# Summing a half's exponentials within that half's own turn of the loop

## The chip, the cores and the metric

The kernel runs on one core of one Trainium2 chip. The metric is the device time of one execution in microseconds. Three executions of the kernel before took 923.88, 924.41 and 924.57 us, a median of 924.41.

## The reference

The program is hashed attention followed by one MLP-mixer block. With 4 batches, 8 heads, 768 positions and 64 values a head, a query sees the keys whose 6-bit hash equals its own:

```python
q_bits = (np.einsum('bhsd,dk->bhsk', q, proj) > 0)
k_bits = (np.einsum('bhsd,dk->bhsk', k, proj) > 0)
mask = q_bucket[:, :, :, None] == k_bucket[:, :, None, :]
scores = np.where(mask, scale * np.matmul(q, k.transpose(0, 1, 3, 2)), -1000000000.0)
attn = np.exp(scores - np.max(scores, axis=-1, keepdims=True))
attn = attn / (np.sum(attn, axis=-1, keepdims=True) + 1e-09)
x = np.matmul(attn, v)
...
h = np.maximum(xt @ w_tok1, 0.0) @ w_tok2      # token mixing
u = x + h.transpose(0, 2, 1)
out = u + np.maximum(u @ w_ch1, 0.0) @ w_ch2   # channel mixing
```

## The kernel before

There are three stages, one behind the other: attention (to about 386 us of the profiled span), token mixing, and channel mixing. The change lies in `attention`. Each engine works through its own instructions in the order in which the code emits them, so that this order is what the change edits; waits between engines are semaphores that the framework adds from the tiles that are read and written.

Attention runs over 16 pairs of heads, `n`, and over two halves of 384 queries for each pair: 32 halves, numbered 0 to 31 here. A half's `scores` (L299) multiplies the six key blocks of 128 keys with its queries on TensorE and adds the hash bits; ScalarE turns each block into an exponential tile `e` (L306). The score banks of PSUM rotate over three buffers, which the hash products share, so that the fourth block waits until ScalarE has read the first.

`add` sums the six `e` tiles of a half. Part 0 adds `e` 0 and 1 on GpSimd into `esa` (L329) and `e` 2, 3, 4 on VectorE into `esd` (L331, L332); part 1 adds `e` 5 (L334) and then `esa` (L335) on VectorE. `sums` sends `esd` through TensorE against a tile of ones (L343); ScalarE takes Ln and Exp of the result (L347, L348), and VectorE refines the reciprocal in two instructions (L350, L351), called the refinement below. `weigh` multiplies the `e` tiles by the values on TensorE (L359), ScalarE copies the result to `num` (L364), and GpSimd multiplies it by the reciprocal into `XT` (L367).

The loop is shifted by one half: during half k (`now`) the sums and the weighing of half k-1 (`before`) run, so on TensorE the order of half k is scores of k, sums of k-1, the hash product of the next pair (L266, in the first half of a pair only), weighing of k-1. VectorE turns the hash products into bits `g` (L271, L274), and the SP queue sends them on in eight small transfers (L280), followed in that queue by the next `qk` (L240), a raw weight tile (L154) and the next values (L248, L250).

Beside all this the 64-bit mixer weights are converted, one tile of 768 columns at a time, in three thirds that are spread over three halves. Third 0, `begin`, scales the low words on ScalarE (L165) and builds the high part on VectorE (L167, L170). Third 1, `join`, masks on VectorE (L182), then multiplies and adds on GpSimd (L185, L186). Third 2, `end`, squares on ScalarE (L195), writes the weight on VectorE (L196), and fetches the next raw tile; there is one raw buffer. Eight tiles pass in the loop. A half in which third 1 is emitted is called a joining half below.

Of the kernel before, what the change touches and what calls it, by code (L numbers as in the profile page):

```python
# [48 lines left out]
def kernel(  # L49
# [169 lines left out]
    def turn(b, x, bank):  # L219

        for r in range(0, NR, 2):
            ps = bank()
            for k in range(2):
                at = S * b + P * (r + k)
                for cb in range(NCB):
                    nc.tensor.transpose(ps[:, k, P * cb : P * cb + P], XT[:, cb, at : at + P], ident)
            nc.scalar.copy(x[:, r : r + 2], ps)


    def attention(pool, psum, W1, W2, x0):  # L230
# [3 lines left out]
        def load_qk(n):  # L234
            if n >= len(pairs):
                return
            b, hp = pairs[n]
            t = pool.tile([P, 2, S], F32, name="qk", tag="qk", bufs=3)
            for sl in [slice(0, HALF), slice(HALF, S)] if n == 0 else [slice(0, S)]:
                nc.sync.dma_start(out=t[:, :, sl], in_=qk[b, hp, :, :, sl])  # L240
            loaded[n] = [t, None, None, None]

        def load_v(n):
            if n >= len(pairs):
                return
            b, hp = pairs[n]
            vn = pool.tile([P, 2, NR, D], F32, name="vn", tag="vn", bufs=3)
            nc.sync.dma_start(out=vn, in_=v[b, hp])  # L248
            vt = pool.tile([P, S], F32, name="vt", tag="vt", bufs=2)
            nc.sync.dma_start(out=vt, in_=vT[b, hp])  # L250
            loaded[n][1:3] = vn, vt

        def add_values(n):

            vt = loaded[n][2]
            vsum = pool.tile([P, 1], F32, name="vsum", tag="vsum", bufs=4)
            nc.scalar.activation(vt, vt, ACT.Copy, scale=-EPS, accum_out=vsum)
            loaded[n][3] = vsum

        def hashes(n):  # L260

            g = pool.tile([P, HALF], BF16, name="g", tag="g", bufs=2)
            ps = psum.tile([P, 2, 512], F32, name="hp", tag="sc", bufs=3)[:, 0]
            for j in range(4):
                sl = slice(HALF * (j // 2), HALF * (j // 2) + HALF)
                nc.tensor.matmul(  # L266
                    ps[32 * j : 32 * j + 32, :HALF], projblk, loaded[n][0][:, j % 2, sl],
                    start=True, stop=True,
                )
            for rows in [slice(0, 64), slice(64, P)] if n == 0 else [slice(0, P)]:  # L270
                nc.vector.tensor_scalar(  # L271
                    g[rows], ps[rows, :HALF], 0.0, 0.5, op0=ALU.is_gt, op1=ALU.subtract,
                )
                nc.vector.tensor_scalar(g[rows], g[rows], bitscale[rows], None, op0=ALU.mult)  # L274
            for j in range(4):
                sl = slice(HALF * (j // 2), HALF * (j // 2) + HALF)
                for i in range(2):
                    at = 32 * j + 16 * i
                    issuer = nc.scalar if n == 0 and i else nc.sync
                    issuer.dma_start(  # L280
                        out=zeroed[n % 3][D * i : D * i + NB + 1, j % 2, sl], in_=g[at : at + NB + 1],
                    )

        class Half:
# [54 lines left out]
            def sums(self):  # L339

                ps = psum.tile([P, 512], F32, name="sums", tag="sm", bufs=1)[:, :HALF]
                for i in range(2):
                    nc.tensor.matmul(  # L343
                        ps[D * i : D * i + D], ones, self.d[:, i], start=True, stop=True,
                    )
                near = pool.tile([P, HALF], F32, name="near", tag="near", bufs=2)
                nc.scalar.activation(near, ps, ACT.Ln)  # L347
                nc.scalar.activation(near, near, ACT.Exp, scale=-1.0)  # L348
                rec = self.rec = pool.tile([P, HALF], F32, name="rec", tag="rec", bufs=2)
                nc.vector.tensor_tensor(rec, ps, near, op=ALU.mult)  # L350
                nc.vector.scalar_tensor_tensor(rec, rec, 2.0, near, op0=ALU.subtract, op1=ALU.mult)  # L351
# [31 lines left out]
        before = None  # L383
        third = 0
        for n in range(len(pairs)):
            for half in range(2):
                now = Half(n, half)
                now.scores()
                if n == half == 0:
                    add_values(0)  # L390
                if before:
                    before.add(1)
                    before.sums()
                if half == 0 and n + 1 < len(pairs):
                    hashes(n + 1)
                    load_qk(n + 2)
                if half == 1 and n + 1 < len(pairs):
                    add_values(n + 1)
                if n:
                    weights.some(third)  # L400
                    third = (third + 1) % 3
                now.add(0)
                if before:
                    before.weigh()
                if half == 0:
                    load_v(n + 2)
                before = now
        while third or weights.fetched:
            weights.some(third)
            third = (third + 1) % 3  # L410
        before.add(1)
        turn(0, x0, lambda: psum.tile([P, 2, 512], F32, name="trp", tag="sc", bufs=3))
        before.sums()
        before.weigh()


# [318 lines left out]
    def attention_and_tokens(W1, W2, x0):  # L735
        inside(attention, W1, W2, x0)
        pool = late.enter_context(tc.tile_pool(name="late", bufs=1, side="right", reuse_waits="tile"))
        WC2 = big["WC2"] = pool.tile([P, NHT, DM], F32, name="WC2")
        SW1 = big["SW1"] = pool.tile([P, 3, NCB // 2, DCH // 2], F32, name="SW1")
        SW2 = big["SW2"] = pool.tile([P, 3, NHT // 2, DM // 2], F32, name="SW2")  # L740

        def weights(pool):
            return Conversion(
                pool, [(w_ch1, WC1, 1, (NCB // 2, NCB)), (w_ch2, WC2, 3, (0, NHT))], bufs=3,
            )

        def jobs(conversion):
            n1, n2 = (NCB // 2) * DCH // NW, NHT * DM // NW
            return [
                *[conversion.one] * (n1 + 1),  # L750
                *weight_sums(
                    WC1, SW1, slice(0, NCB // 2), slice(NCB // 2, NCB),
                    slice(0, DCH // 2), slice(DCH // 2, DCH),
                ),
                *[conversion.one] * n2,
                *weight_sums(
                    WC2, SW2, slice(0, NHT // 2), slice(NHT // 2, NHT),
                    slice(0, DM // 2), slice(DM // 2, DM),
                ),
            ]  # L760

        inside(tokens, W1, W2, x0, weights, jobs)
# [63 lines left out]
```

## Time and profile before

| what | value |
|---|---|
| median of 3 runs | 924.41 us |
| the profiled execution's own time | 924.47 us |
| its span, first to last instruction | 922.6 us |
| TensorE busy in the span | 871.5 us (94%) |
| VectorE, ScalarE, GpSimd busy | 512.3, 323.0, 261.8 us |
| mean granted TensorE clock over the span | 0.98 |

Times in the timeline are counted from the start of the span. "Idle before" is the time that an engine stood still ahead of an instruction, with the instruction that released it. A granted clock of 1.00 is 2.4 GHz; where TensorE is at the lower of its two levels, 1.2 GHz, its matmuls take about twice as long in the timeline.

### The profile page before, as it was taken

The page shows a single profiled execution, that of the slowest core. Times are in us where ns is not written, and L with a number is a line of the kernel's source. Part 1 is how long each engine was busy: PE and PEld are TensorE (multiplying, and loading weights), DVE is VectorE, ACT ScalarE, POOL GpSimd, SP SyncE. Part 2 cuts the span into 40 slices and gives each one's busy share as a digit, 9 for nine tenths or more (in the row PEclk, how much of TensorE's full clock was granted, in tenths as well). Part 3 has the DMA queues.
Part 4 walks back from the last instruction along what each step waited for, and adds up shares of the span by engine and source line. Part 5 has one row for each costly group of instructions (what it writes and reads, how often), then busy time and mean ns, then how long its engine had stood idle before and what let it go on. Part 6 is the DMA issues. An engine that isn't in the chain of part 4 may idle for free.

```text
span 922.6 us, 9203 instructions
## 1 busy us (share of the span) xinstructions
PE 871.5 (94%) x3505; PEld 397.0 (43%) x3505; DVE 512.3 (56%) x576; ACT 323.0 (35%) x477; POOL 261.8 (28%) x156
## 2 busy tenths in 40 slices
PE   5989889889889899999999999999999999999997
PEld 1434334334334444545553444444444444444443
DVE  1675776666675756558996447353446452335511
ACT  2656666666656565543421220101121101221000
POOL 3343553551651532254652111110111110111020
PEclk8999999989999999999999999999999999999999
DMA  4222222322312220221320120131110110000001
GB/s 173 72 71 106 105 71 106 104 71 105 105 71 105 71 71 3 103 69 68 118 88 1 69 69 0 58 114 65 61 68 35 57 69 34 0 1 0 23 23 49
DMA packets 20499, 61.14 MB, mean 66 GB/s; under 512 B 2784, under 2 KB 4192, under 8 KB 20448
## 3 DMA queue, kind: packets, MB, share of 16 engines
q1 hardware_dynamic: 20392, 60.46, 18.5%
q8 instruction: 29, 0.48, 0.2%
q14 instruction: 22, 0.18, 0.1%
q10 hardware_dynamic: 56, 0.02, 0.0%
HBM read 53.49 MB, written 6.29 MB: 65 GB/s over the span
## 4 chain that ended last, share of the span: by engine, by line
PE 75%; DVE 9%; POOL 7%; ACT 3%; DMA 2%; SPq 2%; issue 1%; DVEq 0%; ACTq 0%
PE b L581 46%; PE sc L299 10%; PE acc L359 8%; PE t L516 4%; PE sums L343 3%; POOL tmp L185 2%; POOL tmp L186 2%; PE t L529 2%; POOL esa L329 2%; DVE esd L335 2%; SPq L280 1%; DMA raw<-in_moe_w_tok 1%; PE hp L266 1%; DMA qk<-in_qk 1%; DVE tmp L170 1%
## 5 line engine op out<-in xcount | busy, mean ns | idle before, releaser
L306 ACT ACTIVATE e<-sc 128x768 f32<-128x768 f32 x192 | 151.8, 812 | 29.7 <-PE sc L299 29.6
L299 PE MATMUL sc<-qk 64*128 64x384 f32 x768 | 160.5, 497 | 1.0 <-ACT e L306 1.0
L588 ACT COPY p<-b 128x512 f32<-128x512 f32 x72 | 42.2, 586 | 295.5 <-PE b L581 295.5
L359 PE MATMUL acc<-e,vn 128*64 128x384 f32 x768 | 136.5, 507 | 0.0
L581 PE MATMUL b<-r,WC 128*128 128x512 f32 x288 | 125.6, 592 | 0.0
L581 PE MATMUL b<-T,SW 128*128 128x512 f32 x216 | 97.0, 593 | 1.7 <-DVE T L671 0.9
L607 POOL TENSOR_TENSOR p<-p,p 128x512 f32<-128x512 f32 x18 | 25.4, 1414 | 238.9 <-ACT p L588 228.2
L299 PEld LDWEIGHTS sc<-qk 64*128 64x128 f32 x768 | 67.5, 189 | 58.4 <-issue 47.8
L359 PEld LDWEIGHTS acc<-e,vn 128*64 128x64 f32 x768 | 56.5, 143 | 79.7 <-issue 77.9
L581 PEld LDWEIGHTS b<-r,WC 128*128 128x128 f32 x288 | 54.7, 190 | 68.9 <-issue 66.5
L367 POOL TENSOR_TENSOR XT<-num,rec 128x384 f32<-128x384 f32 x32 | 41.0, 1280 | 145.4 <-ACT num L364 141.5
L329 POOL TENSOR_TENSOR esa<-e 128x768 f32<-128x768 f32 x32 | 73.0, 2281 | 29.3 <-ACT e L306 29.3
L350 DVE TENSOR_TENSOR rec<-sums,near 128x384 f32<-128x384 f32 x32 | 17.9, 558 | 101.3 <-ACT near L348 101.3
L185 POOL TENSOR_TENSOR tmp<-tmp,raw 128x768 f32<-128x768 f32 x20 | 46.2, 2309 | 91.7 <-DVE tmp L182 54.6
L581 PE MATMUL b<-T,WC 128*128 128x512 f32 x144 | 67.7, 593 | 0.1
L299 PE MATMUL sc<-bits 64*128 64x384 bf16 x384 | 63.6, 325 | 1.3 <-DMA bits<-g 1.3
L581 PE MATMUL b<-XT,WC 128*128 128x512 f32 x144 | 64.7, 592 | 0.0
L581 PEld LDWEIGHTS b<-T,SW 128*128 128x128 f32 x216 | 40.9, 190 | 54.0 <-issue 50.5
L581 PE MATMUL b<-r,SW 128*128 128x512 f32 x144 | 62.8, 592 | 0.0
L611 DVE TENSOR_TENSOR r<-p,u 128x512 f32<-128x512 f32 x18 | 12.5, 692 | 87.6 <-ACT u L588 87.0
L343 PE MATMUL sums<-esd,ones 128*64 128x384 f32 x128 | 31.1, 568 | 28.4 <-DVE esd L335 28.4
L335 DVE SCALAR_TENSOR_TENSOR esd<-esd,esa 128x768 f32<-128x768 f32 x32 | 42.6, 1330 | 16.1 <-POOL esa L329 13.6
(81 smaller groups left out, 992.8 us busy)
## 6 DMA issues: line engine op xcount, KB each, us to landing
raw<-in_moe_w_ch SPq DMA_DIRECT2D x16, 768.0 KB
seen<-in_qk SPq DMA_DIRECT2D x16, 768.0 KB
qk<-in_qk SPq DMA_DIRECT2D x15, 768.0 KB
vn<-in_v SPq DMA_DIRECT2D x16, 384.0 KB
vt<-in_vT SPq DMA_DIRECT2D x16, 384.0 KB
out<-p SPq DMA_DIRECT2D x18, 256.0 KB
raw<-in_moe_w_tok SPq DMA_DIRECT2D x4, 768.0 KB
bits<-g SPq DMA_DIRECT2D x124, 5.2 KB
```

What stands on the lines that cost most here:

```text
L185: nc.gpsimd.tensor_tensor(unit, unit, lo, op=ALU.mult)
L299: nc.tensor.matmul(sc[:, i, :HALF], t[rows, 1, P * c : P * c + P], t[rows, 0, qs], start=start, stop=not start,)
L306: nc.scalar.activation(e, sc[:, :, :HALF], ACT.Exp, scale=SCALE)
L329: nc.gpsimd.tensor_tensor(self.a, es[0], es[1], op=ALU.add)
L335: nc.vector.scalar_tensor_tensor(self.d, self.d, NR * EPS, self.a, op0=ALU.add, op1=ALU.add,)
L343: nc.tensor.matmul(ps[D * i : D * i + D], ones, self.d[:, i], start=True, stop=True,)
L359: nc.tensor.matmul(acc[D * i : D * i + D], vn[:, i, c], e[:, i], start=(c == 0), stop=(c == NR - 1),)
L367: nc.gpsimd.tensor_tensor(XT[:, hp, at : at + HALF], num, self.rec, op=ALU.mult)
L516: nc.tensor.matmul(ps, W1[:, r, P * j : P * j + P], x[:, r], start=(r == 0), stop=(r == NR - 1),)
L581: nc.tensor.matmul(self.ps[i], left(k), right(k), start=first and k == ks[0], stop=k == ks[-1], skip_group_check=True,)
L588: nc.scalar.copy(c, self.ps[i])
L607: nc.gpsimd.tensor_tensor(p7, p5, p7, op=ALU.add)
```

## The change

`now.add(0)` moves from the end of a half's turn, behind the weight third, to a place straight behind its scores. `now.add(1)` moves from the next half's turn into the half's own: it stands behind the refinement of half k-1, ahead of the weight third. So that the refinement can be placed by itself, it is cut off `sums` into a method of its own, `newton`, which stands behind the hash bits. No instruction is added or removed.

```diff
--- before.py
+++ after.py
@@ -346,6 +346,10 @@
                 near = pool.tile([P, HALF], F32, name="near", tag="near", bufs=2)
                 nc.scalar.activation(near, ps, ACT.Ln)
                 nc.scalar.activation(near, near, ACT.Exp, scale=-1.0)
+                self.ps, self.near = ps, near
+
+            def newton(self):
+                ps, near = self.ps, self.near
                 rec = self.rec = pool.tile([P, HALF], F32, name="rec", tag="rec", bufs=2)
                 nc.vector.tensor_tensor(rec, ps, near, op=ALU.mult)
                 nc.vector.scalar_tensor_tensor(rec, rec, 2.0, near, op0=ALU.subtract, op1=ALU.mult)
@@ -388,18 +392,20 @@
                 now.scores()
                 if n == half == 0:
                     add_values(0)
+                now.add(0)
                 if before:
-                    before.add(1)
                     before.sums()
                 if half == 0 and n + 1 < len(pairs):
                     hashes(n + 1)
                     load_qk(n + 2)
                 if half == 1 and n + 1 < len(pairs):
                     add_values(n + 1)
+                if before:
+                    before.newton()
+                now.add(1)
                 if n:
                     weights.some(third)
                     third = (third + 1) % 3
-                now.add(0)
                 if before:
                     before.weigh()
                 if half == 0:
@@ -408,9 +414,9 @@
         while third or weights.fetched:
             weights.some(third)
             third = (third + 1) % 3
-        before.add(1)
         turn(0, x0, lambda: psum.tile([P, 2, 512], F32, name="trp", tag="sc", bufs=3))
         before.sums()
+        before.newton()
         before.weigh()
```

On VectorE, a joining half without a hash product and the half behind it, with one. `tmp` and `W_93` belong to the weight thirds, `rec` to the refinement, `g` to the hash bits. Before:

```order
L182 TENSOR_SCALAR tmp<-tmp 128x768
L331 TENSOR_TENSOR esd<-e 128x768
L332 TENSOR_TENSOR esd<-esd,e 128x768
L334 TENSOR_TENSOR esd<-esd,e 128x768
L335 SCALAR_TENSOR_TENSOR esd<-esd,esa 128x768
L350 TENSOR_TENSOR rec<-sums,near 128x384
L351 SCALAR_TENSOR_TENSOR rec<-rec,near 128x384
L271 TENSOR_SCALAR g<-hp 128x384
L274 TENSOR_SCALAR g<-g,bitscale 128x384
L196 SCALAR_TENSOR_TENSOR W_93<-raw,tmp 128x768
```

After (the refinement's two lines are now L354 and L355):

```order
L334 TENSOR_TENSOR esd<-esd,e 128x768
L335 SCALAR_TENSOR_TENSOR esd<-esd,esa 128x768
L182 TENSOR_SCALAR tmp<-tmp 128x768
L331 TENSOR_TENSOR esd<-e 128x768
L332 TENSOR_TENSOR esd<-esd,e 128x768
L271 TENSOR_SCALAR g<-hp 128x384
L274 TENSOR_SCALAR g<-g,bitscale 128x384
L354 TENSOR_TENSOR rec<-sums,near 128x384
L355 SCALAR_TENSOR_TENSOR rec<-rec,near 128x384
L334 TENSOR_TENSOR esd<-esd,e 128x768
L335 SCALAR_TENSOR_TENSOR esd<-esd,esa 128x768
L196 SCALAR_TENSOR_TENSOR W_93<-raw,tmp 128x768
```

Before, the joining half's four additions stand behind L182; now all four stand ahead of it, and the next half's first two stand ahead of the bits and the refinement.

On GpSimd, the same joining half with what stands ahead of it and behind it. Before:

```order
L367 TENSOR_TENSOR XT<-num,rec 128x384
L185 TENSOR_TENSOR tmp<-tmp,raw 128x768
L186 TENSOR_TENSOR tmp<-tmp 128x768
L329 TENSOR_TENSOR esa<-e 128x768
L367 TENSOR_TENSOR XT<-num,rec 128x384
L329 TENSOR_TENSOR esa<-e 128x768
```

After (L371 is the former L367):

```order
L329 TENSOR_TENSOR esa<-e 128x768
L185 TENSOR_TENSOR tmp<-tmp,raw 128x768
L186 TENSOR_TENSOR tmp<-tmp 128x768
L371 TENSOR_TENSOR XT<-num,rec 128x384
L329 TENSOR_TENSOR esa<-e 128x768
L371 TENSOR_TENSOR XT<-num,rec 128x384
```

The joining half's own addition has moved from behind the two instructions of the join to ahead of them; the addition of the half behind it still follows them. The orders of TensorE and of ScalarE are as before.

## Rows read from the trace of the kernel before

**Rows 1.** Waits, 20 to 440 us: engine, line <- releaser: total us, times, longest us
```profile
PE sums L343 <- DVE esd L335: 28.4, 12, 3.2
...
DVE esd L335 <- POOL esa L329: 13.6, 8, 1.7
```

**Rows 2.** Busy us (x instructions) of each engine by stretch, granted clock, DMA share, GB/s
```profile
28.00:323.00 295.00, 266.58 (x1698) 118.75 (x1696) 195.02 (x206) 182.34 (x268) 129.47 (x67) 0.95 0.25 91
...
323.00:374.00 51.00, 51.00 (x344) 23.30 (x340) 28.93 (x34) 33.98 (x51) 16.45 (x11) 1.00 0.10 34
...
199.00:209.00 10.00, 6.82 (x32) 2.06 (x30) 5.50 (x7) 4.13 (x6) 6.26 (x4) 0.68 0.01 2
```

**Rows 3.** Timeline of TensorE, sums products: start us, us, engine, line, names, [idle before <-releaser]
```profile
28.35 0.87 PE L343 MATMUL sums<-esd,ones 128*64 128x384 f32 x4
...
132.65 0.87 PE L343 MATMUL sums<-esd,ones 128*64 128x384 f32 x4 [3.18 <-DVE esd L335]
...
155.02 0.87 PE L343 MATMUL sums<-esd,ones 128*64 128x384 f32 x4 [1.31 <-DVE esd L335]
...
203.65 1.55 PE L343 MATMUL sums<-esd,ones 128*64 128x384 f32 x4 [3.19 <-DVE esd L335]
...
343.81 0.87 PE L343 MATMUL sums<-esd,ones 128*64 128x384 f32 x4
...
354.45 0.87 PE L343 MATMUL sums<-esd,ones 128*64 128x384 f32 x4
...
364.16 0.87 PE L343 MATMUL sums<-esd,ones 128*64 128x384 f32 x4
...
373.88 0.87 PE L343 MATMUL sums<-esd,ones 128*64 128x384 f32 x4
...
381.70 0.87 PE L343 MATMUL sums<-esd,ones 128*64 128x384 f32 x4 [0.31 <-DVE esd L335]
```

**Rows 4.** Timeline: a raw weight transfer that comes late for ScalarE
```profile
136.64 3.70 SPq L280 DMA_DIRECT2D bits<-g  x5
...
143.14 0.36 SPq L154 DMA_DIRECT2D raw<-in_moe_w_tok  x1
...
147.96 0.92 PE L299 MATMUL sc<-qk 64*128 64x384 f32 x4
...
148.86 0.94 ACT L165 ACTIVATE raw<-raw 128x768 f32<-128x768 uint32 x1 [2.78 <-DMA raw<-in_moe_w_tok]
...
151.01 0.92 PE L299 MATMUL sc<-qk 64*128 64x384 f32 x4 [0.36 <-ACT e L306]
```

**Rows 5.** Timeline of GpSimd and VectorE in one joining half and its successor
```profile
194.37 2.48 POOL L185 TENSOR_TENSOR tmp<-tmp,raw 128x768 f32<-128x768 f32 x1 [6.18 <-DVE tmp L182]
...
195.19 2.48 DVE L332 TENSOR_TENSOR esd<-esd,e 128x768 f32<-128x768 f32 x1
...
196.94 2.41 POOL L186 TENSOR_TENSOR tmp<-tmp 128x768 f32<-128x768 f32 x1
...
201.86 1.73 DVE L335 SCALAR_TENSOR_TENSOR esd<-esd,esa 128x768 f32<-128x768 f32 x1 [1.70 <-POOL esa L329]
```

**Rows 6.** Groups by line, 60 to 460 us: busy us, mean ns | idle before
```profile
L331 DVE TENSOR_TENSOR esd<-e 128x768 f32<-128x768 f32 x28 | 26.6, 951 | 0.0
...
L182 DVE TENSOR_SCALAR tmp<-tmp 128x768 uint32<-128x768 uint32 x16 | 8.9, 557 | 0.3
```

**Rows 7.** Timeline, all engines, single instructions that price the new order
```profile
221.71 0.92 PE L299 MATMUL sc<-qk 64*128 64x384 f32 x4
...
222.91 4.76 ACT L306 ACTIVATE e<-sc 128x768 f32<-128x768 f32 x6 [0.44 <-PE sc L299]
...
226.75 0.87 PE L343 MATMUL sums<-esd,ones 128*64 128x384 f32 x4
...
228.75 0.56 DVE L350 TENSOR_TENSOR rec<-sums,near 128x384 f32<-128x384 f32 x1 [2.11 <-ACT near L348]
...
393.30 1.84 POOL L185 TENSOR_TENSOR tmp<-tmp,raw 128x768 f32<-128x768 f32 x1 [5.12 <-ACT raw L165]
```

## The prediction

> **What bounds the kernel now.** I read the waits first, then TensorE's timeline, then the queues of the engine it waits for. In attention TensorE stands still 28.4 us ahead of the sums product, always for L335, the last addition on VectorE, and L335 itself waits eight times for GpSimd's `esa` [rows 1]. From 28 to 323 us TensorE lacks that much of being busy throughout (266.6 of 295 us), at a mean granted clock of 0.95; from 323 to 374 us, where no weight is converted, it is busy all the time at 1.00 [rows 2]. TensorE bounds the stage, then, and what it loses lies where weights are converted.
>
> How much it loses, clock included, I take from the starts of the sums products [rows 3]. In the undisturbed stretch one half with a hash product takes 354.45 - 343.81 = 10.64 us, one without 373.88 - 364.16 = 9.71. From the first sums product (28.35) to that of half 31 (373.88) there are 30 halves, 14 of them with a hash product: 14 x 10.64 + 16 x 9.71 = 304.3 us. The trace has 345.5. So 41.2 us are lost, 28.1 of them as those waits (0.31 of the 28.4 lie behind 373.88, at 381.70), 0.36 as a wait for an exponential [rows 4], and the other 12.7 mainly at the lower clock: behind its wait of 3.19 us the sums product at 203.65 takes 1.55 us instead of 0.87 [rows 3], and the mean clock of that stretch is 0.68, so part of it ran at 1.2 GHz [rows 2]. Not every wait is followed by this: behind 3.18 us at 132.65 and 1.31 us at 155.02 the product still takes 0.87 [rows 3].
>
> **Why L335 is late.** In a joining half the trace shows the two engines taking turns [rows 5]. L332 starts at 195.19 while GpSimd's L185 runs to 196.85, and ends 0.82 us later; L186 starts at 196.94, gets going when L332 has ended at 197.67, and ends 1.68 us later. So an instruction of 0.95 us on VectorE [rows 6] takes 2.48 beside GpSimd. Behind the join, GpSimd still has this half's `esa`, the previous half's `XT` and the next `esa`, and L335 at 201.86 has waited 1.70 us for the first of these before its own turn.
>
> **What the change does to that, laid out in time.** No instruction is added, so only places count. Let t = 0 be the first score product of a joining half H without a hash product. From the undisturbed half at 221.71 [rows 7]: the exponentials end from t = 2.0 on, 0.79 apart, the last at 6.0 (4.76 us from 222.91); TensorE reaches the sums at 5.04 (226.75) and the next scores at 9.71; the refinement can start at 7.04 (228.75). VectorE's wide additions take 0.95, the halves of the refinement 0.56 each, the mask L182 0.56 [rows 6, 7]; GpSimd's L185, alone, takes 1.84 [rows 7], and I give L186 and `esa`, of the same shape, the same.
>
> - Half H: GpSimd adds `esa` from 2.85 to 4.7. VectorE runs L331 and L332 to 6.4, the refinement 7.05 to 8.15, L334 and L335 to 10.1, L182 to 10.65. TensorE wants this half's sum at 9.71 + 5.04 = 14.75: 4.6 us to spare.
> - The join: L185 from 10.75 to 12.6, L186 to 14.45, in a gap in which VectorE has nothing of its own, since the next L331 needs an exponential that ends at 9.71 + 4.4 = 14.1.
> - Half H+1, with a hash product: L331, waiting its turn, 14.45 to 15.3; `XT` to 16.2; L332 to 17.05; `esa` to 18.7. The hash product ends near 16.4, so L271 could start at 17.05; waiting its turn behind `esa`, it ends at 19.15, L274 at 19.5. Refinement to 20.7, L334 to 21.65, `XT` of H, L335 near 23.5. Wanted at 20.35 + 5.04 = 25.4: 1.9 us to spare, where the trace before is 3.1 us late.
>
> With the hash product in H instead of H+1 the same sums leave about 2 us. The whole 41.2 us therefore should go, together with the 0.31 us ahead of the last sums product. What hides the moved work is TensorE's own weighing and scores; without that cover each us by which L335 passes its mark is a us of TensorE, eight times.
>
> **What is late next** is the raw weight. Third 2's L196 now stands behind L335, and in the SP queue the raw fetch stands behind the hash bits. L196 is done at 24.4; the fetch is reached 6.5 us after the first bit transfer (136.64 to 143.14 [rows 4]), that is at about 25.8, so L196 is covered, and the bits set it. Before, the bits left 3.99 us behind the sums product (136.64 - 132.65 [rows 3, 4]). Now they leave at 19.6, 4.85 behind it (14.75), if L271 waits for its turn, and at 19.1, 4.35, if it does not (no row shows an instruction that reads PSUM beside GpSimd). Four of the eight fetches follow a third 2 in a first half, and ScalarE's L165 of the next half waits for them, with `num` and the next exponentials queued behind it: at 148.86, 0.90 us past the first score product at 147.96, this cost TensorE the 0.36 us at 151.01 [rows 4]. Later by 0.36 to 0.86, it costs 0.7 to 1.2, and up to 1.7 if the transfer takes half a us more. The other such fetches were hidden by the very stalls that go. I take 1.1, four times: 4.4 us, between 2.9 and 6.9. The fetches behind a second half are issued at 24.4, not behind bits, and at the 5.7 us of 143.14 to 148.86 land near 30.1, before the next scores at 31.0; they cost nothing, or what they are late.
>
> One rule bears on the choice for L271. The Trainium skill, "GPSIMD Engine Reference", section "1. Specifications", says that GpSimd's SBUF interfaces are shared with VectorE and that it contends with VectorE instructions that run in a 2-port mode or have two SBUF inputs. The turns of the additions agree with it (0.95 us to 2.48 [rows 5, 6]); L271 reads one operand, from PSUM, and by the rule would not wait: 4 x 0.75 = 3.0 us would replace the 4.4, and the time would be 886.0.
>
> The sum, against the profiled execution's own 924.47: 924.47 - 41.2 - 0.3 + 4.4 = **887.4**, from 885.9 to 889.9. That execution stands 0.06 above the median of the runs shown, so I write 887.3.
>
> **The rivals.**
> - Raw weights no later than now. If the bits leave as before, at most the 0.36 us comes four times: 883.0 to 884.4. For it: VectorE reads the hash product ahead of the refinement, not behind it. Against it: `esa` now falls into the same moment.
> - A rest of the stall. If in the half behind a join VectorE meets two more GpSimd instructions than I laid out (2 x 1.68 = 3.4 us [rows 5]), the 1.9 us are gone and 1.5 remain in each of eight halves, too short to be sure of a lower clock [rows 3]: +12, 899. For it: spare time is small, and all six additions and `XT` crowd there. Against it: GpSimd has nothing more to do in that half.
> - Slower than before. The refinement now stands ahead of L334 and L335, so one half's sum hangs on the previous half's: sums product, 2.0 us to the refinement (226.75 to 228.75 [rows 7]), 1.15, 1.9 for the two additions, about 5.1 in all, against 10.15 us a half. If each of the four instructions waits out a GpSimd instruction, it is 5.1 + 4 x 1.68 = 11.8, and each of 30 halves loses 1.65: 887 + 49 = 936. It decides from a loop of 10.15 on, that is three such waits in every half. Against it: GpSimd is busy 129 us of 295 there [rows 2].
> - The change doesn't do what it says: the sum still ends with the join, because the next half's `esa` stands behind it as before, and the eight waits of about 3.1 us just move on by one half: 924, within 0.2%. Against it: L185 starts at t = 10.75, some 6 us ahead of that `esa`'s turn.
>
> **How the numbers follow.** Forecast 0.63, raw weights no later 0.18, a rest of the stall 0.12, slower 0.04, no effect 0.03. The likeliest gives 887.3. The range takes in the forecast, the first rival with a us for what the gaps of the trace leave open, and the smaller part of the second (up to 1.1 us a join): 882.0 to 896.0; some 0.15 lies outside. A measurement of this kernel can tell about 0.2% from no change. Faster by more than that 0.93, within it 0.03, slower 0.04.
>
> **What would show it.** Right: the wait of the sums product for L335 falls from 28.4 us to under 2; the starts of sums products lie 9.71 and 10.64 us apart nearly everywhere from 28 us on; the clock of the converting stretch is near 1.00; the join's L185 starts about 10.7 us after its half's first score product. New: waits of the scores for exponentials of 0.7 to 1.7 us, four times, each behind an L165 that waited for a raw tile. Wrong: sums products that still wait in halves behind a join, refinements starting over 1 us after their Exp has ended in most halves, or score waits above 2 us. A start of bit transfers other than 4.35 to 4.85 us behind the sums product shows that my choice for L271 failed.

## The result, and the profile after

| | kernel before | changed kernel |
|---|---|---|
| median of 4 runs each | 924.49 us (923.88 to 926.23) | 885.88 us (885.13 to 887.87) |
| profiled execution, its span | 924.47 us, 922.6 us | 885.13 us, 883.2 us |
| mean granted clock over the span | 0.98 | 0.995 |
| ratio | | 0.9583, 95% interval 0.9562 to 0.9604 |

The changed kernel is 4.2% faster. The forecast was 887.3 us, in a range of 882.0 to 896.0.

First the busy time of each engine from the page of the changed kernel.

```profile
PE 861.0 (97%) x3505; PEld 394.2 (45%) x3505; DVE 494.6 (56%) x576; ACT 321.4 (36%) x477; POOL 243.8 (28%) x156
```

TensorE is busy 97% of the span. Now the waits of TensorE and VectorE from 20 to 440 us; the columns are those of [rows 1].

```profile
PE sc L299 <- ACT e L306: 1.8, 4, 0.9
...
DVE esd L331 <- ACT e L306: 87.8, 31, 4.4
DVE rec L354 <- ACT near L348: 10.7, 14, 4.5
```

The wait of the sums product for the last addition, 28.4 us in [rows 1], is gone altogether. Four short waits of the scores for an exponential, 1.8 us, are what is left. On VectorE the wait that shrank is that of the refinement for its Exp: in the kernel before it was

```profile
DVE rec L350 <- ACT near L348: 101.3, 32, 6.0
```

and it is 10.7 us now, because the additions that used to stand behind the refinement run while it waits. VectorE now stands 87.8 us ahead of the next half's L331 instead, and TensorE doesn't wait for that. The stretch and the starts of sums products that answer to [rows 2, 3]:

```profile
28.00:323.00 295.00, 293.21 (x1952) 133.09 (x1954) 200.56 (x234) 205.40 (x305) 123.71 (x73) 1.00 0.27 97
...
27.93 0.87 PE L343 MATMUL sums<-esd,ones 128*64 128x384 f32 x4
68.64 0.87 PE L343 MATMUL sums<-esd,ones 128*64 128x384 f32 x4
79.52 0.87 PE L343 MATMUL sums<-esd,ones 128*64 128x384 f32 x4
335.22 0.87 PE L343 MATMUL sums<-esd,ones 128*64 128x384 f32 x4
```

From the first sums product to that of half 31 it is 335.22 - 27.93 = 307.3 us, where [rows 3] have 345.5: 38.2 us less. The rest of the 39.4 us by which the spans differ is 0.4 us ahead of the first sums product, 0.4 us ahead of the last one, and 0.4 us behind it. Of the 307.3 us, 304.3 are the 30 halves at TensorE's own pace; the other 3.0 us lie in four halves like that from 68.64 to 79.52, which takes 10.88 us instead of 9.71.

### The profile page after: what moved, and what is told of

Its sections match the earlier page's. It is cut to its first block, busy times and chain, and to the rows that moved or that the text cites. A ratio compares the mean times of both kernels' runs of the same rounds, so it can differ in the third digit from the quotient of the medians.

```text
span 883.2 us, 9198 instructions
## 1 busy us (share of the span) xinstructions
PE 861.0 (97%) x3505; PEld 394.2 (45%) x3505; DVE 494.6 (56%) x576; ACT 321.4 (36%) x477; POOL 243.8 (28%) x156
## 3 DMA queue, kind: packets, MB, share of 16 engines
q1 hardware_dynamic: 20392, 60.46, 19.8%
## 4 chain that ended last, share of the span: by engine, by line
PE 90%; DVE 4%; DMA 2%; ACT 1%; issue 1%; SPq 1%; POOL 0%; DVEq 0%; ACTq 0%
PE b L587 48%; PE sc L299 16%; PE acc L363 13%; PE t L522 4%; PE sums L343 3%; PE t L535 2%; PE hp L266 2%; DMA qk<-in_qk 1%; PE trp L226 1%; SPq L280 1%; DMA raw<-in_moe_w_tok 1%; DVE XT L541 1%; DVE WC L196 1%; DVE tmp L170 1%; ACT e L306 1%
## 5 line engine op out<-in xcount | busy, mean ns | idle before, releaser
L363 PE MATMUL acc<-e,vn 128*64 128x384 f32 x768 | 130.0, 488 | 0.0
L331 DVE TENSOR_TENSOR esd<-e 128x768 f32<-128x768 f32 x32 | 41.2, 1289 | 93.5 <-ACT e L306 93.5
L363 PEld LDWEIGHTS acc<-e,vn 128*64 128x64 f32 x768 | 53.9, 137 | 72.4 <-issue 72.2
L329 POOL TENSOR_TENSOR esa<-e 128x768 f32<-128x768 f32 x32 | 66.4, 2076 | 33.7 <-ACT e L306 33.7
L371 POOL TENSOR_TENSOR XT<-num,rec 128x384 f32<-128x384 f32 x32 | 39.1, 1221 | 125.8 <-ACT num L368 87.5
L185 POOL TENSOR_TENSOR tmp<-tmp,raw 128x768 f32<-128x768 f32 x20 | 41.0, 2052 | 86.0 <-DVE tmp L182 48.8
L368 ACT ACTIVATE num<-acc,vsum 128x384 f32<-128x384 f32 x32 | 18.6, 580 | 71.2 <-PE acc L363 71.2
L535 PE MATMUL t<-W,r 128*128 128x384 f32 x128 | 42.3, 488 | 1.6 <-DVE XT L541 1.6
```

The source lines that it names most:

```text
L185: nc.gpsimd.tensor_tensor(unit, unit, lo, op=ALU.mult)
L329: nc.gpsimd.tensor_tensor(self.a, es[0], es[1], op=ALU.add)
L331: nc.vector.tensor_tensor(self.d, es[2], es[3], op=ALU.add)
L363: nc.tensor.matmul(acc[D * i : D * i + D], vn[:, i, c], e[:, i], start=(c == 0), stop=(c == NR - 1),)
L371: nc.gpsimd.tensor_tensor(XT[:, hp, at : at + HALF], num, self.rec, op=ALU.mult)
L535: nc.tensor.matmul(ps[:, :HALF], r1[:, j, P * cb : P * cb + P], W2[:, j, HALF * half : HALF * half + HALF], start=(j == 0), stop=(j == NJ ...
```

## The experiments

Each run is compared with runs of the kernel before on the same chip, whose medians lie between 925.3 and 926.9 us. Part 0 and part 1 of the additions, the third and the refinement are named as ahead of the prediction.

### Which part of the change did it

**Only GpSimd's addition moved.** `esa` goes straight behind the scores, ahead of the join; VectorE's order is that of before.

```diff
                 now.scores()
...
+                now.add_a()          # esa <- e0 + e1 on GpSimd
...
                 now.add(0)           # now only L331, L332
```

> The kernel before, with only GpSimd's esa addition moved to straight behind the scores, ahead of the join; VectorE's order stays. My theory (both the queue position of esa and the meeting of VectorE's additions with the join cost time): L335 no longer waits for esa, but L332, L334 and L335 still take turns with L185, L186 and XT, and end about 1.5 us past the mark instead of 3.1; eight waits of 1.5 us, little or no time at the lower clock: 893 to 901 us. Rival (the place of esa alone was the cause): about 886 us and no wait of the sums product.

Measured: 920.15 us against 926.85, ratio 0.9926 (0.9897 to 0.9955). Both theories missed. TensorE's wait, three of its sums products, and what stands ahead of two of them (in this kernel's lines L346 is the sums product, L338 the last addition and L327 `esa`):

```profile
PE sums L346 <- DVE esd L338: 28.0, 23, 2.8
...
47.02 2.16 POOL L327 TENSOR_TENSOR esa<-e 128x768 f32<-128x768 f32 x1 [0.33 <-ACT e L306]
47.61 2.38 DVE L338 SCALAR_TENSOR_TENSOR esd<-esd,esa 128x768 f32<-128x768 f32 x1
50.04 0.87 PE L346 MATMUL sums<-esd,ones 128*64 128x384 f32 x4 [0.79 <-DVE esd L338]
61.25 0.87 PE L346 MATMUL sums<-esd,ones 128*64 128x384 f32 x4 [1.43 <-DVE esd L338]
78.03 0.56 DVE L167 TENSOR_SCALAR tmp<-raw 128x768 uint32<-128x768 uint32 x1 [2.54 <-DMA raw<-in_moe_w_tok]
85.73 0.87 PE L346 MATMUL sums<-esd,ones 128*64 128x384 f32 x4 [2.78 <-DVE esd L338]
```

The wait behind the joining half does fall, from about 3.1 to 1.43 us at 61.25, as expected. But the total wait is 28.0 us as before, in 23 pieces instead of 12. At 85.73 it is 2.78 us, in a half whose additions stand behind a raw tile that came late (L167 at 78.03 has waited 2.54 us for it). The 0.79 us at 50.04 fall ahead of the first join: the last addition of that half now meets the next half's `esa`, which used to stand behind the join, and takes 2.38 us, where the kernel before has 0.96 (at 47.13). What was gained, 6.7 us, is clock: 0.98 in the stretch from 28 to 323 us, where [rows 2] have 0.95.

**Only VectorE's first two additions moved.** The mirror image: L331 and L332 go straight behind the scores, `esa` stays behind the join.

```diff
                 if before:
                     before.add(1)
+                now.add(0)           # L331, L332 only
+                if before:
                     before.sums()
...
-                now.add(0)
+                now.add_a()          # esa, still behind the third
```

> The kernel before, with only VectorE's first two additions of a half (L331, L332 of before) moved to straight behind the scores; esa stays behind the join on GpSimd, and the last two additions stay in the next half's turn. My theory: esa ends at about 14.9 us after the half's first score product (mask at 8.75, L185 and L186 to 13.1, esa behind them) and the last addition at 15.8, where it is wanted at 14.75: eight waits of about 1 us, full clock: 891 to 897 us. Rival (VectorE's places alone matter): about 886 us.

Measured: 909.67 us against 926.85, ratio 0.9813 (0.9785 to 0.9842). Eight waits there are, but of 1.8 us and not of 1, and four waits of the scores of 0.7 to 2.9 us that were not expected:

```profile
PE sums L346 <- DVE esd L338: 14.6, 8, 1.9
PE sc L299 <- ACT e L306: 7.4, 4, 2.9
...
125.11 1.73 DVE L338 SCALAR_TENSOR_TENSOR esd<-esd,esa 128x768 f32<-128x768 f32 x1 [5.39 <-POOL esa L327]
126.90 0.87 PE L346 MATMUL sums<-esd,ones 128*64 128x384 f32 x4 [1.88 <-DVE esd L338]
132.32 5.90 SPq L280 DMA_DIRECT2D bits<-g  x8
144.57 0.56 DVE L167 TENSOR_SCALAR tmp<-raw 128x768 uint32<-128x768 uint32 x1 [3.89 <-DMA raw<-in_moe_w_tok]
```

L338 at 125.11 has waited 5.39 us for `esa` and holds up VectorE for it, the hash bits among what is behind: they leave 5.4 us behind the sums product (132.32 - 126.90) instead of 4.0, the raw tile is fetched at 138.82 and used at 144.57. So the two moves need each other: alone they give 6.7 and 17.2 us; with both of them, and the refinement behind the bits, the next run has 40.4.

**Part 1 put back.** The changed kernel, with L334 and L335 in the next half's turn again.

```diff
+                if before:
+                    before.add(1)
                 now.add(0)
...
-                now.add(1)
```

> The changed kernel, with part 1 of the additions (L334, L335) put back into the next half's turn, ahead of its part 0; part 0 stays straight behind the scores, the refinement stays behind the bits. My theory (what counts is that esa stands ahead of the join and that the additions meet it less): the last addition still ends before its mark, since only one third's instructions on VectorE stand ahead of it: 884 to 888 us. Rival (all additions have to lie in the half's own turn): waits of 1 us and more in eight halves, 893 us or more.

Measured: 886.46 us against 926.85, ratio 0.9563 (0.9535 to 0.9591), and no wait of the sums product at all. The changed kernel, beside it in the table at the end of this section, takes 885.77. The move of part 1, half of the diff, neither gives nor takes anything that can be measured here. The gain lies in the rest, the move of part 0 and that of the refinement behind the bits. What the refinement's place is worth by itself no run shows. An estimate: ahead of the bits its two instructions (0.56 us each [rows 7]) would hold the bits up by about 1.1 us, and with them the four raw tiles that TensorE comes to wait for, so up to some 4.5 us.

**Part 0 ahead of the third only.** One line of the kernel before moved: `now.add(0)` stands just ahead of the weight third, still behind the bits and the refinement.

```diff
+                now.add(0)
                 if n:
                     weights.some(third)
                     third = (third + 1) % 3
-                now.add(0)
```

> The kernel before with one line moved: part 0 of the additions stands just ahead of the weight third instead of just behind it; refinement and bits stay ahead of it, part 1 stays in the next half's turn. It tells the place ahead of the weight third from the place ahead of the refinement and the bits. My theory (what counts is to stand ahead of the third on both engines): L332 ends near 10.9 us after the half's first score product, the last addition at 14.5 to 15 where it is wanted at 14.75: waits of 0 to 0.5 us, 885 to 893 us. Rival (the additions must stand ahead of the refinement too): eight waits of 1 us or more, 896 us or more.

Measured: 897.92 us against 925.31, ratio 0.9703 (0.9653 to 0.9752): outside what my theory expected, 885 to 893. TensorE's wait, and the half behind a join:

```profile
PE sums L343 <- DVE esd L335: 11.8, 13, 1.1
...
66.27 1.76 DVE L196 SCALAR_TENSOR_TENSOR W<-raw,tmp 128x768 f32<-128x768 f32 x1
68.10 2.47 POOL L329 TENSOR_TENSOR esa<-e 128x768 f32<-128x768 f32 x1 [0.88 <-ACT e L306]
69.00 2.38 DVE L335 SCALAR_TENSOR_TENSOR esd<-esd,esa 128x768 f32<-128x768 f32 x1
71.44 0.87 PE L343 MATMUL sums<-esd,ones 128*64 128x384 f32 x4 [1.04 <-DVE esd L335]
```

VectorE still stands 89.0 us ahead of the refinement, with its additions queued behind. Part 1, behind all of these and the third (L196 here), comes so late that it meets the next half's `esa`: L335 takes 2.38 us instead of 0.96, and the sum is 1.04 us late. 13 waits of 0.3 to 1.1 us are left. But for the 0.31 us ahead of the last sum they lie in halves with third 0 or third 2; the joining halves, whose third has only the 0.55 us of L182 on VectorE, have none. Going ahead of the third on both engines is worth 27 of the 39 to 40 us; going ahead of the refinement and the bits, with the refinement behind the bits, the other 11 to 13 (897.9 to 886.5 with part 1 put back, two chips).

### What the join and the raw tiles have to do with it

**The join left out.** The kernel before without L185 and L186 in attention; the low words of the weights converted there are missing from the result.

```diff
-            nc.gpsimd.tensor_tensor(unit, unit, lo, op=ALU.mult)
-            nc.gpsimd.tensor_tensor(big, big, unit, op=ALU.add)
```

> The kernel before, with the join's two GpSimd instructions (L185, L186) left out in attention, so that the low words of the weights converted there are missing; all else stays. My theory: the join on GpSimd is the cause of all long waits, directly and through the clock, so without it the order of before runs as the changed one: 884 to 888 us, clock of the converting stretch near 1.00. Rival (VectorE's thirds or the raw transfers cause part of the waits): 895 us or more, with waits of the sums product left in joining halves.

Measured: 911.27 us against 926.85, ratio 0.983 (0.98 to 0.9861). The theory of the prediction, that the join makes the waits, holds for a part only: 15.6 us go with it, and 18.6 us of waiting remain.

```profile
PE sums L344 <- DVE esd L336: 18.6, 14, 2.8
...
75.59 0.56 DVE L167 TENSOR_SCALAR tmp<-raw 128x768 uint32<-128x768 uint32 x1 [2.93 <-DMA raw<-in_moe_w_tok]
77.06 0.95 DVE L332 TENSOR_TENSOR esd<-e 128x768 f32<-128x768 f32 x1
79.72 2.45 DVE L335 TENSOR_TENSOR esd<-esd,e 128x768 f32<-128x768 f32 x1
83.29 0.87 PE L344 MATMUL sums<-esd,ones 128*64 128x384 f32 x4 [2.80 <-DVE esd L336]
```

The sums product at 83.29 waits 2.80 us, and not behind a join: L167 at 75.59 has waited 2.93 us for its raw tile, and the additions, which stand behind the third in this order, begin at 77.06 behind it and then meet `XT` and `esa`. That the stalls behind the join gave these tiles time in the kernel before is argued from this; the run with two raw buffers alone, below, bears it out.

**The same with two raw buffers.** A second buffer lets the next tile be fetched in third 0, two halves earlier.

```diff
-            if k == 2:
+            if k == 0:
                 self.fetch()
...
-            raw = self.pool.tile([P, NW, 2], U32, name="raw", tag="raw", bufs=self.bufs)
+            raw = self.pool.tile([P, NW, 2], U32, name="raw", tag="raw", bufs=max(self.bufs, 2))
```

> The kernel before without the join's two GpSimd instructions in attention (the low words of those weights are missing), and with two raw weight buffers, the next tile fetched in third 0. My theory now: in the order of before, the additions of a half stand behind the weight third on VectorE, so a raw tile that comes late holds them up too; the four waits of 2.8 us of the sums product and the four of the scores that the version without the join still had (13 us) go, the waits of 0.8 to 0.9 us stay: 894 to 900 us. Rival (those waits come from XT and esa on GpSimd alone): 908 us or more.

Measured: 895.36 us against 925.31, ratio 0.9675 (0.9626 to 0.9724). The waits of 2.8 us and those of the scores are gone; 13 waits of 0.3 to 1.1 us are left, 11.3 us in sum.

```profile
PE sums L344 <- DVE esd L336: 11.3, 13, 1.1
...
47.41 2.38 DVE L336 SCALAR_TENSOR_TENSOR esd<-esd,esa 128x768 f32<-128x768 f32 x1
49.85 0.87 PE L344 MATMUL sums<-esd,ones 128*64 128x384 f32 x4 [0.79 <-DVE esd L336]
```

So even with no join and no late tile, the order of before loses some 10 us. The refinement alone doesn't do it: where no weight is converted, the same order waits nowhere but 0.31 us ahead of the last sum. All other waits lie in halves in which third 0 (1.5 us of L167 and L170 on VectorE) or third 2 (0.96 us) stands ahead of the additions too; they then meet `XT` and the next half's `esa`.

**Two raw buffers alone,** in the kernel before.

> The kernel before with two raw weight buffers, the next tile fetched in third 0. My theory: the long waits behind the join were also what gave the raw tiles time, so taking the raw tiles' lateness away gains little by itself: the eight waits of about 3 us stay, 917 to 925 us. Rival (late raw tiles are a cause of their own beside the join): the gain of the version without the join, some 13 us, comes here too: 912 us or less.

Measured: 924.83 us against 925.31, ratio 0.9968 (0.9935 to 1.0001): no difference that can be told. The eight waits of about 3 us stay, as expected:

```profile
PE sums L343 <- DVE esd L335: 26.0, 10, 3.2
```

While the join is there, late tiles cost nothing that can be told; without it they cost 14 to 16 us (by the ratios 0.983 and 0.9675, and by the times 911.27 and 895.36).

### What is left, and how much room there is

**Two raw buffers in the changed kernel,** beside the changed kernel itself on the same chip, five runs each.

> The changed kernel again, beside the next one on the same chip: 885 to 887 us.

> The changed kernel with two raw weight buffers in attention, the next tile being fetched in third 0 (about two halves earlier) instead of third 2. My theory: the four waits of the scores for an exponential, behind ScalarE's first weight instruction and its raw tile, are what is left of the stage over TensorE's own time (307.3 against 304.3 us); they go, and the time falls by 2.5 to 3.3 us. Rival (ScalarE is late there for another reason, or the transfers now meet others): within 1 us of the changed kernel.

| five runs each | median | lowest to highest | ratio to before |
|---|---|---|---|
| changed kernel | 885.77 us | 885.6 to 886.9 | 0.9576 (0.9562 to 0.9589) |
| with two raw buffers | 882.30 us | 881.48 to 883.39 | 0.9532 (0.9519 to 0.9545) |

The four waits go, and 3.5 us with them (2.5 to 3.3 expected). The stretch of this version:

```profile
28.00:332.00 304.00, 304.00 (x2032) 138.95 (x2030) 208.65 (x240) 215.86 (x317) 127.58 (x77) 1.00 0.26 94
```

TensorE is busy 304.00 of 304.00 us at a granted clock of 1.00; in this stretch the order of the other engines has nothing more to give. It is the fastest version here, 0.4% ahead of the changed kernel.

**The join issued twice and three times** in the changed kernel, the extra pairs writing to a tile that nothing reads any more: 3.65 and 7.3 us more of GpSimd in each of eight halves.

```diff
             nc.gpsimd.tensor_tensor(big, big, unit, op=ALU.add)
+            nc.gpsimd.tensor_tensor(unit, big, lo, op=ALU.mult)
+            nc.gpsimd.tensor_tensor(unit, big, lo, op=ALU.add)
```

> The changed kernel with GpSimd's two join instructions issued twice in attention (the second pair writes to a tile that nothing reads any more): 3.65 us more of GpSimd in each of eight halves. My theory: the last addition of the half behind a join ends 2.4 to 3.7 us ahead of its mark in the changed kernel, part of the extra work falls into GpSimd's idle time, and 1 to 2 us stay spare: no wait of the sums product, 885 to 889 us. Rival (the room is used up): eight waits of 1 us or more, 894 us or more.

> As the one before with the two join instructions issued three times: 7.3 us more of GpSimd in each of eight halves. My theory: esa of the half behind a join now ends past the mark; sums products wait about 1.5 to 2.5 us in eight halves: 896 to 906 us, more if the clock falls. Rival (GpSimd is off the path altogether): within 2 us of the changed kernel.

Measured: 903.08 us for two (ratio 0.9759, 0.9737 to 0.9781), 927.35 for three (1.0021, 1.0007 to 1.0036), against 925.53. Both cost more than expected. For two, the sums products hold, but the scores don't:

```profile
PE sums L346 <- DVE esd L338: 1.1, 4, 0.3
PE sc L302 <- ACT e L309: 13.6, 7, 3.1
...
67.53 2.57 DVE L199 SCALAR_TENSOR_TENSOR W<-raw,tmp 128x768 f32<-128x768 f32 x1
70.16 0.38 SPq L154 DMA_DIRECT2D raw<-in_moe_w_tok  x1
75.84 0.91 ACT L165 ACTIVATE raw<-raw 128x768 f32<-128x768 uint32 x1 [5.07 <-DMA raw<-in_moe_w_tok]
77.97 0.92 PE L302 MATMUL sc<-qk 64*128 64x384 f32 x4 [2.62 <-ACT e L309]
```

Third 2's write, L199 in this kernel, ends at 70.1 instead of 66.6 (L196 of the changed kernel, at 64.86); the raw fetch has to wait for it at 70.16, ScalarE gets its tile at 75.84, and TensorE stands 2.62 us for an exponential. To show that the raw tile is the way, **both together,** the doubled join and the second buffer:

> The changed kernel with GpSimd's two join instructions issued twice, and two raw weight buffers, the next tile fetched in third 0. My theory: the 17 us that the doubled join cost were late raw tiles (the last third ends later, so the fetch does), not late sums: 882 to 888 us with sums products waiting at most 0.3 us. Rival (the doubled join is in the way of the sums or of XT): 895 us or more.

Measured: 890.34 us against 925.31, ratio 0.9621 (0.9569 to 0.9673): between the two, and no wait of the scores is left. With the second buffer the doubling costs 8.0 us (890.34 against 882.30), without it 17.3 (903.08 against 885.77), so 9.3 of the 17.3 us were late tiles. But now sums products do wait, 7.9 us in seven pieces of up to 1.58. The room behind the join is used up by 3.65 us of GpSimd, and with one buffer the wait for tiles had hidden it. For three, the eight sums products wait 28.6 us in sum and the time is that of the kernel before: the gain hangs on GpSimd's share of the work as much as on the order.

## Why the prediction was right

**The loss of 41.2 us, clock included.** It was read as the difference between the halves as they were and the halves of the undisturbed stretch, and this is what came: 345.5 us became 307.3, and with two raw buffers the whole stretch runs at TensorE's pace. A sum over waits alone (28.4 us) would have missed a third of it.

**The layout of a joining half.** Laid against the trace of the changed kernel for H with t = 0 at 43.24 (the sums product at 48.28, less 5.04), and H+1 with a hash product:

```profile
53.28 0.55 DVE L182 TENSOR_SCALAR tmp<-tmp 128x768 uint32<-128x768 uint32 x1
53.91 1.84 POOL L185 TENSOR_TENSOR tmp<-tmp,raw 128x768 f32<-128x768 f32 x1 [5.97 <-DVE tmp L182]
55.83 1.81 POOL L186 TENSOR_TENSOR tmp<-tmp 128x768 f32<-128x768 f32 x1
57.33 1.12 DVE L331 TENSOR_TENSOR esd<-e 128x768 f32<-128x768 f32 x1 [3.50 <-ACT e L306]
59.28 2.55 POOL L329 TENSOR_TENSOR esa<-e 128x768 f32<-128x768 f32 x1
60.05 0.55 DVE L271 TENSOR_SCALAR g<-hp 128x384 bf16<-128x384 f32 x1
60.63 1.31 DVE L274 TENSOR_SCALAR g<-g,bitscale 128x384 bf16<-128x384 bf16 x1
61.98 5.90 SPq L280 DMA_DIRECT2D bits<-g  x8
63.98 0.96 DVE L335 SCALAR_TENSOR_TENSOR esd<-esd,esa 128x768 f32<-128x768 f32 x1
```

L182 ends at t = 10.6 (10.65 forecast), L185 begins at 10.67 (10.75), L186 ends at 14.4 (14.45), L331 at 15.2 (15.3). L335 ends at 64.94, 3.7 us ahead of the sums product at 68.64 (1.9 forecast); in the half behind a join that has no hash product it is 2.4 us (about 2 forecast). The step of this layout that failed is L271: I let it wait its turn behind `esa`, and at 60.05 it takes 0.55 us in the midst of an `esa` that runs from 59.28 to 61.83. So the refinement was done 0.9 us earlier than laid out (t = 19.8, 20.7 forecast) and L335 1.8 us (21.7, 23.5 forecast): `XT` of H, laid out ahead of L335, begins only at 64.43, with L335 under way.

**The raw weights.** The end of the chain is as forecast: the raw tile, ScalarE's L165 behind it, the next exponentials, a wait of the scores, in four halves where the kernel before has one.

```profile
68.48 0.39 SPq L154 DMA_DIRECT2D raw<-in_moe_w_tok  x1
74.75 0.94 ACT L165 ACTIVATE raw<-raw 128x768 f32<-128x768 uint32 x1 [3.33 <-DMA raw<-in_moe_w_tok]
76.90 0.92 PE L299 MATMUL sc<-qk 64*128 64x384 f32 x4 [0.90 <-ACT e L306]
```

Its beginning is not, and its size was put too high: 3.0 us measured for 4.4 (2.9 to 6.9). The bits do not leave later than before. In all four halves it is 3.95 to 3.98 us behind the sums product (61.98 - 58.00 here), against 3.99 before and 4.35 to 4.85 forecast, which by the prediction's own last paragraph shows the choice for L271 wrong; the rest is L274, which is done 0.11 us behind `esa` (61.94 and 61.83) and not a whole instruction behind it. So the tiles come no later than they did, and what is new is that the stalls no longer hide three of the four. The waits are 0.90, 0.37, 0.21 and 0.32 us, the longest behind the one tile that took 6.2 us to land (68.48 to 74.67) instead of 5.5 to 5.7, and each of the four halves is 0.27 us longer than its wait, which the forecast had not counted.

With L271 not waiting, the prediction gave 886.0 by the rule of the Trainium skill's "GPSIMD Engine Reference", section "1. Specifications"; the trace agrees with the rule in this point (0.55 us beside `esa`). That the median is 885.9 is in part luck: none of the four halves costs the 0.75 us of that sum, but 1.17, 0.64, 0.48 and 0.59.

**The rivals.** The first, raw weights no later than now, had its condition met; its 883.0 to 884.4 was too low, since it gave a wait 0.36 us at most. The refinement ahead of the additions is no bound: the loop it closes is not seen as a wait anywhere. The join doesn't just move on. Of the second rival, a rest of the stall, nothing is there, but the runs with the doubled join show how near it was: 3.65 us more of GpSimd a join brings 7.9 us of it, once the tiles are on time.

**Where the reasoning was too narrow.** The prediction took the join for the cause of the loss, and the number came out because the change removes more than that. The runs show three things that the order of before made late one behind the other, each hidden while a longer one stood in front: the join (15.6 us come back when it is left out), late raw tiles that held up the additions on VectorE (another 14 to 16 once the join is out, none that can be told while it is there), and additions that start only when the refinement and VectorE's part of the third are done (some 10 us with neither of the others). The change takes the additions out from behind all three at once, so the step "Why L335 is late" named only the longest of them. That the prediction judged the whole time against a stretch without any of them, and not cause by cause, is why this did no harm to the number; the cause behind it was right in part only.

## What to carry to other kernels

On an in-order queue, put work in the order in which its operands become ready: the additions had theirs some 2 us ahead of the refinement, and the refinement, the bits and the third stood in front of them. Where several waits hide one another, don't add up a gain for each cause: take the time of a stretch in which none of them occurs as the bound, and expect any single fix to bring out the next one. Look at what a late instruction at the end of a chain releases (here the fetch into a single buffer) before it is called hidden.

## What the runs showed of the hardware

VectorE and GpSimd take turns only for some instructions. In the run with part 0 ahead of the third alone, both halves of the refinement fall beside one `esa`:

```profile
61.43 1.82 POOL L329 TENSOR_TENSOR esa<-e 128x768 f32<-128x768 f32 x1
61.67 0.56 DVE L350 TENSOR_TENSOR rec<-sums,near 128x384 f32<-128x384 f32 x1 [2.85 <-ACT near L348]
62.27 1.40 DVE L351 SCALAR_TENSOR_TENSOR rec<-rec,near 128x384 f32<-128x384 f32 x1
```

L350, with one input in PSUM and one in SBUF, takes its usual 0.56 us; L351, with both in SBUF, is held until `esa` has ended at 63.25 and takes 1.40. The same stands above for L271 (PSUM, 0.55) and L274 (SBUF, bf16, 1.31 instead of 0.32).

A wait of TensorE is not always followed by the lower clock, and its length alone does not tell. In the run with only VectorE's additions moved, two sums products waited 1.87 us (at 59.46) and 1.88 us (at 126.90). Behind the first, part of the stretch ran at 1.2 GHz: the mean granted clock is 0.76, and the weighing takes 5.53 us instead of the usual 4.09. From 126 to 133 us, behind the second, the clock is 1.00.

```profile
59.00:66.00 7.00, 6.54 (x34) 2.35 (x36) 6.83 (x9) 1.83 (x3) 2.08 (x1) 0.76 0.00 1
```

Waits of 2.8 to 3.9 us were sometimes followed by it, sometimes not. The sums product itself is no sure sign, as the prediction took it to be: in the kernel before, the one at 61.68, behind 3.18 us, takes its usual 0.87, but the hash product behind it 1.36 instead of 0.85, and the clock from 61 to 70 us is 0.81. Behind the one at 132.65, which the prediction names, the clock did hold (1.00 from 131 to 143 us).

It can change from one execution to the next. The kernel before with two raw buffers ran eight times, six times in 924.5 to 925.8 us at a mean clock of 0.974 or 0.975 and twice in 916.8 and 917.3 at 0.989: the same program, 8 us apart. That the clock alone makes the difference is not shown, since no trace of the faster ones exists.
